# Gate logits of layer 1's row blocks: the gate's columns stationary in four column quarters, and one product that adds and turns

## The chip, the cores and the metric

One core of one Trainium2 chip runs the whole program. The metric is the device time of one launch in microseconds. Three runs of the kernel before took 630.59, 631.4 and 633.81 us, a median of 631.4.

## The reference

Chunked attention (2 batches, 8 heads, 768 positions) gives 1536 rows of 512 numbers. These go through two mixture layers of 8 experts each, whose weights are 512x1024 and 1024x512.

```python
logits = x @ w_gate                                   # layer 1, with a noise term; each row keeps its best 2 experts
h = np.maximum(x[mask] @ w1[e], 0.0)
out[mask] += top2_w[mask, k, None] * (h @ w2[e])

logits = x @ w_gate                                   # layer 2: x is layer 1's output; each row goes to its best expert
expert_idx = np.argmax(logits, axis=1)
probs = softmax(logits);  gate_w = probs[rows, expert_idx]
disp[e, counts[e]] = x[i]                             # up to `capacity` rows per expert, in row order
h = np.maximum(einsum('ecd,edf->ecf', disp, w1), 0.0);  y = einsum('ecf,efd->ecd', h, w2)
out[i] = gate_w[i] * y[expert_idx[i], pos[i]]
```

The second gate is linear in layer 1's output, so the kernel computes its logits for every expert's part of a row and lets the transfer that adds the parts in memory add the logits too.

## The kernel before, in words

**Jobs.** The expert work is a list of jobs that run one after the other: `V0`, `V8`, then `S[0]` to `S[6]` (layer 1), then `U0`, `UL` and seven more (layer 2). A job has units. A job of kind "M" has 8 units `layer1` (one 128-wide slice of the hidden layer each) and then, for each block of 128 rows, two units `rows` (the halves of the second product). `V0` is of kind "T" with one block of rows. `V8` and `S[0]` to `S[3]` are of kind "W", whose output has the rows as columns; they take their logits in `y_block` and the change doesn't touch them. `S[4]`, `S[5]` and `S[6]` are of kind "M" with three blocks of rows each. With `V0` that makes ten row blocks in layer 1.

**A row block's end.** After the second `rows` unit, `weighted` (ScalarE, L873) writes the block times its gate into `yr`. Two steps go onto a list `todo`: `row_columns` (L876) transposes `yr` on TensorE (L881) and copies the result to `yt` on ScalarE (L882); `put` calls `row_logits` and `scatter`. `row_logits` multiplies four 128x128 slices of `yt`, stationary, by the gate's 8 columns, moving, in plain fp32 into one PSUM bank (L888), and VectorE copies the 8 logits behind the row in `yr` (L889). `scatter` (L891) is an indirect transfer from GpSimd's queue that adds the block's rows to `x2_rows` in memory (L895).

**When a step runs.** `run_jobs` takes one step off `todo` after each unit in a job of kind "M" or "W" (none after the first unit, except in `S[0]`, `S[6]` and `U0`), and only steps that were there before the unit. All engines run their instructions in the order in which they were written. At the end of `S[6]` the list is emptied down to one step, which runs after `U0`'s first unit.

**What hangs on the logits.** The routing of layer 2 runs in the background in small pieces between the big products: `choose` (from unit 3 of `S[5]`), `early` (from unit 3 of `S[6]`) and `late` (from unit 3 of `U0`). Each first loads all logits with one transfer on SP's queue (L1470), which waits for all scatters written before it; then VectorE works on them (L393 on) and TensorE ranks them (L1525 in `early`, L1557 in `late`). The big products are `mm3` (L811): each operand is split into a rounded part and the rest, and three of the four products are taken; the weights come in halves that are loaded (`raww`), rounded on ScalarE (`whi`, L745) and subtracted on VectorE (`wlo`, L746). The other lines that the prediction speaks of are in the attention at the start: L242 (scores: a stationary operand of 128 rows and 64 columns, whose output goes to the lower and the upper half of the partitions in turn), L283 (64 rows and 32 columns, four places in turn), L308 (transposes) and L318 (gate logits of layer 1, of the same form as L888 but for 18 moving columns). All of these are plain fp32; in the trace such a product has two weight loads and two matmul records, and a transpose has one of each.

Of the kernel before, what the change touches and what calls it, by code (L numbers as in the profile page):

```python
# [8 lines left out]
F32 = mybir.dt.float32  # L9
# [4 lines left out]
AF = mybir.ActivationFunctionType  # L14
OP = mybir.AluOpType
AX = mybir.AxisListType
# [38 lines left out]
def attention_two_moe_kernel(  # L55
# [7 lines left out]
    nc = tc.nc  # L63
    B, H, S, D = q.shape
    NM = mem_k.shape[2]
    DM, E = w_gate1.shape
# [6 lines left out]
    KD = DM // 128  # L73
# [4 lines left out]
    W2 = DM + 8  # L78
# [24 lines left out]
    def bank(tag):  # L103
        return ps["p"].tile([128, 512], F32, name="ps" + tag, bufs=2)
# [68 lines left out]
    ident = consts.tile([128, 128], F32, name="ident")  # L173
# [10 lines left out]
    xb, st = {}, {}  # L184
# [3 lines left out]
    wg2 = consts.tile([128, KD, E], F32, name="wg2")  # L188
# [521 lines left out]
    wp = {}  # L710
# [149 lines left out]
    def rows2(n0, blk, half_, C, between=None):  # L860

        n = min(128, C - 128 * blk)
        s_ = slice(128 * blk, 128 * blk + n)
        if half_ == 0:
            st["l2"] = bank("C")
        hh, hl = st["h"]
        w = P[n0 + 2 + half_]
        mm3(st["l2"][:n], [((hh[:, 4 * half_ + f, s_], hl[:, 4 * half_ + f, s_]), (w[0][:, f], w[1][:, f]))
                           for f in range(4)], half_ == 0, half_ == 1, between, RO)

    def weighted(ps, g, n):
        yr = wp["B"].tile([128, W2], F32, name="yr", bufs=3)
        nc.scalar.activation(yr[:n, 0:DM], ps[:n], AF.Copy, scale=g[:n])  # L873
        return yr

    def row_columns(yr, n):  # L876

        p = bank("B")
        pv = p.rearrange("p (k n) -> p k n", k=KD)
        for k in range(KD):  # L880
            nc.tensor.transpose(pv[:, k, 0:n], yr[:n, 128 * k:128 * k + 128], ident[:n, :n])  # L881
        nc.scalar.activation(st["yt"][:, :, 0:n], pv[:, :, 0:n], AF.Copy)  # L882

    def row_logits(yr, n):

        p = bank("D")
        for k in range(KD):
            nc.tensor.matmul(p[:n, 0:E], st["yt"][:, k, 0:n], wg2[:, k], start=k == 0, stop=k == KD - 1)  # L888
        nc.vector.tensor_copy(yr[:n, DM:W2], p[:n, 0:E])  # L889

    def scatter(yr, n, ids_ap, first, prev):  # L891
        off = bass.IndirectOffsetOnAxis(ap=ids_ap[:n], axis=0)
        nc.gpsimd.memset(spacer, 0.0)
        if first:
            wr = nc.gpsimd.indirect_dma_start(out=x2_d, out_offset=off, in_=yr[:n], in_offset=None,  # L895
                                              compute_op=OP.add)
        else:
            wr = nc.gpsimd.indirect_dma_start(out=out, out_offset=off, in_=yr[:n, 0:DM], in_offset=None,  # L898
                                              bounds_check=N - 1, oob_is_err=False)
        for z in prev:  # L900
            tc.declare_no_dep(wr.ins, z.ins, reason="rows of other tokens")
        prev.append(wr)
# [39 lines left out]
    class Job:  # L942
# [39 lines left out]
        def rows(self, blk, half_, between=None):  # L982
            rows2(self.n0, blk, half_, self.C, between)
            if half_ == 0:
                return
            n = min(128, self.C - 128 * blk)
            yr = weighted(st["l2"], self.g[blk], n)
            if self.first:
                def put():
                    row_logits(yr, n)  # L990
                    scatter(yr, n, self.ids[blk], True, self.prev)
                self.todo += [lambda: row_columns(yr, n), put]
                return
            f = lambda: scatter(yr, n, (self.oids or self.ids)[blk], False, self.prev)
            if self.oids is None:
                self.later.append(f)
            else:
                f()
# [61 lines left out]
    def picked(b_, fl, idf, nb):  # L1060

        nv = V
        key = b_.tile([128, nv, nb], F32, name="okey")
        codes = b_.tile([128, nv * nb], F32, name="ocode")
        nc.gpsimd.iota(codes, pattern=[[-1, nv * nb]], base=nv * nb, channel_multiplier=0,
                       allow_small_or_imprecise_dtypes=True)
        cv = codes.rearrange("p (e n) -> p e n", e=nv)
        nc.vector.tensor_tensor(key, fl, cv, op=OP.mult)
        mx = b_.tile([128, 1], F32, name="omx")
        nc.vector.tensor_reduce(mx, key, axis=AX.XY, op=OP.max)  # L1070
        nc.vector.tensor_scalar(key, cv, mx[:, 0:1], None, op0=OP.is_equal)
        nc.vector.tensor_tensor(fl, fl, key, op=OP.subtract)
        se = b_.tile([128, nv], F32, name="ose")
        nc.vector.tensor_reduce(se, key, axis=AX.X, op=OP.add)
        idr = b_.tile([128, 2], F32, name="oidr")
        tr = b_.tile([128, nv, nb], F32, name="otr")
        nc.vector.tensor_tensor(tr, key, trash[:, None, 0:nb].to_broadcast([128, nv, nb]), op=OP.mult)
        nc.vector.tensor_reduce(idr[:, 1:2], tr, axis=AX.XY, op=OP.add)
        nc.vector.tensor_tensor(key, key, idf, op=OP.mult)
        nc.vector.tensor_reduce(idr[:, 0:1], key, axis=AX.XY, op=OP.add)  # L1080
        idi = b_.tile([128, 1], I32, name="oidi")
        nc.vector.tensor_tensor(idi, idr[:, 0:1], idr[:, 1:2], op=OP.add)
        return se, idr[:, 0:1], idi
# [9 lines left out]
    def rest1(wa, wb, ov, en, nb, after):  # L1093

        fl, idf, nvi = ov
        n = nc.values_load(nvi[0:1, 0:1], min_val=0, max_val=V * nb)
        b_ = wp["C"]
        with tc.If(n > 0):  # L1098
            with tc.For_i(0, n):
                se, _, idi = picked(b_, fl, idf, nb)  # L1100
                r = expert_of(b_, se, en)
                xg = b_.tile([128, 4, 256], F32, name="oraw", bufs=1).rearrange("p k f -> p (k f)")
                gather(x_d, idi[:, 0:1], xg[:, 0:W1])
                x_block(xg, 0, 128)
                g = wp["A"].tile([128, 1], F32, name="gs", bufs=10)
                gate1(xg, se, g)
                hi, lo = st["y"]

                def part(src):

                    raw = b_.tile([128, 4, 256], F32, name="oraw", bufs=1)
                    nc.sync.dma_start(raw, src)
                    nc.scalar.activation(hi[:, :, 0:256], raw, AF.Copy)
                    nc.vector.tensor_tensor(lo[:, :, 0:256], raw, hi[:, :, 0:256], op=OP.subtract)
                    return [(hi[:, k, 0:256], lo[:, k, 0:256]) for k in range(4)]

                xh, xl = st["x"]
                for f in range(4):
                    ws = part(wa[ds(r, 1)].rearrange("e (k p) f -> p (e k) f", p=128)[:, :, 256 * f:256 * f + 256])
                    ps = bank("A")  # L1120
                    mm3(ps[:, 0:256], [((xh[:, k, 0:128], xl[:, k, 0:128]), ws[k]) for k in range(KD)])
                    nc.scalar.activation(st["hr"][:, 256 * f:256 * f + 256], ps[:, 0:256], AF.Relu)
                for c in range(2):
                    turn(c, 128)
                hh, hl = st["h"]
                ps = bank("C")
                for c in range(2):
                    for j in range(2):
                        ws = part(wb[ds(r, 1)].rearrange("e (k p) f -> p (e k) f", p=128)
                                  [:, 4 * j:4 * j + 4, 256 * c:256 * c + 256])  # L1130
                        mm3(ps[:, 256 * c:256 * c + 256],
                            [((hh[:, 4 * j + k, 0:128], hl[:, 4 * j + k, 0:128]), ws[k]) for k in range(4)],
                            j == 0, j == 1)
                yr = weighted(ps, g, 128)
                row_columns(yr, 128)
                row_logits(yr, 128)
                scatter(yr, 128, idi[:, 0:1], True, [])
            after()

# [131 lines left out]
    n = 0  # L1271
# [88 lines left out]
    st["h"] = (wp["B"].tile([128, FB, CM], F32R, name="hh"), wp["B"].tile([128, FB, CM], F32R, name="hl"))  # L1360
    st["hr"] = wp["B"].tile([128, FF], F32, name="hr")
    st["yt"] = wp["B"].tile([128, KD, 128], F32, name="yt")
    st["y"] = (wp["B"].tile([128, KD, CM], F32R, name="yh"), wp["B"].tile([128, KD, CM], F32R, name="yl"))

    n2 = 4 * E
    kind1 = lambda c: "W" if c > 384 else "M"
    S = [Job(kind1(caps1[1 + s]), 4 + 4 * s, caps1[1 + s], True) for s in range(E - 1)]
# [303 lines left out]
    for job in jobs[1:-1]:  # L1671
        n = job.n0
# [60 lines left out]
```

## Time and profile before

| what | value |
|---|---|
| median of three runs | 631.4 us (630.59 to 633.81) |
| the profiled execution | 632.0 us |
| its span in the trace | 630.2 us |
| TensorE busy | 595.4 us (94%) |
| TensorE weight loads busy | 540.9 us (86%) |
| VectorE busy | 384.1 us (61%) |
| ScalarE busy | 311.2 us (49%) |
| GpSimd busy | 165.0 us (26%) |
| matmul records of L888 | 80 (8 for each of ten row blocks) |

Times in the trace count from the span's start. The 1.8 us between the span and the time of the execution lie around the span. A matmul record lasts until its last result is out, so records of consecutive matmuls overlap, and the distance from one start to the next is what a matmul costs a full engine. "Idle before" in brackets at the end of a row is the time in which that engine had nothing to run, and the arrow names what ended it.

### The profile page before, as it was taken

The numbers are of one execution on the slowest core, as the hardware profiler recorded it, in microseconds if no ns is written. First come the engines' busy times: TensorE is split into PE (matmuls) and PEld (weight loads), VectorE is DVE, ScalarE is ACT, GpSimd is POOL, SyncE is SP. The second block draws the span as 40 slices with busy tenths as digits, with TensorE's granted clock in tenths as the row PEclk, the third lists the DMA queues.
The fourth block names the chain that finished last, engine by engine and source line by source line (L and its number), as shares of the span: only waits on it lengthen the run. The fifth ranks groups of instructions, "written<-read, shape, count | busy, mean of one in ns | idle before, by whom it ended". The sixth has DMA issues, their size and how long they took to land. (4 is left out here: it accounts for less than half of the span.)

```text
span 630.2 us, 12317 instructions
## 1 busy us (share of the span) xinstructions
PE 595.4 (94%) x4523; PEld 540.9 (86%) x4529; DVE 384.1 (61%) x1015; ACT 311.2 (49%) x653; POOL 165.0 (26%) x237
## 2 busy tenths in 40 slices
PE   7699869699999999999999999999999999999996
PEld 4688657499999999999999898988979988889984
DVE  8577754677645555555555447273557648687672
ACT  5265543225544544545445435344427557686563
POOL 8894000211411312313212130302351121111201
PEclk9799886899999999999999999999999999999999
DMA  9986670339775664856536565455366486776751
GB/s 252 269 142 197 214 234 20 88 99 345 222 221 168 174 185 149 221 152 135 170 103 151 166 142 165 107 121 151 38 235 215 152 264 220 251 273 234 247 182 41
DMA packets 77068, 112.13 MB, mean 178 GB/s; under 512 B 28353, under 2 KB 28353, under 8 KB 77000
## 3 DMA queue, kind: packets, MB, share of 16 engines
q1 hardware_dynamic: 68088, 88.99, 44.7%
q0 software_dynamic: 8912, 22.28, 15.7%
q8 instruction: 38, 0.62, 0.4%
q14 instruction: 30, 0.25, 0.1%
HBM read 88.90 MB, written 22.34 MB: 176 GB/s over the span
## 5 line engine op out<-in xcount | busy, mean ns | idle before, releaser
L746 DVE TENSOR_TENSOR wlo<-raww,whi 128x512 fp32r<-128x512 f32 x254 | 168.8, 688 | 44.1 <-ACT whi L745 42.7
L745 ACT ACTIVATE whi<-raww 128x512 fp32r<-128x512 f32 x256 | 152.2, 624 | 17.7 <-DMA raww<-in_moe_w_dram 14.9
L823 DVE SCALAR_TENSOR_TENSOR hl<-psA,hh 128x384 fp32r<-128x384 f32 (+6 forms) x104 | 54.0, 519 | 80.4 <-ACT hh L822 80.0
L822 ACT ACTIVATE hh<-psA 128x384 fp32r<-128x384 f32 (+6 forms) x104 | 47.7, 458 | 109.2 <-PE psA L811 109.2
L811 PE MATMUL psA<-xh,wlo 128*128 128x256 f32 (+6 forms) x416 | 85.8, 328 | 0.8 <-ACT xh L762 0.4
L811 PE MATMUL psA<-xh,whi 128*128 128x256 f32 (+6 forms) x416 | 83.7, 322 | 0.0
L811 PE MATMUL psA<-xl,whi 128*128 128x256 f32 (+6 forms) x416 | 83.6, 323 | 0.0
L895 POOL DMA_INDIRECT x_rows<-yr,ids x25 | 39.2, 1568 | 125.4 <-ACT whi L745 86.2
L811 PEld LDWEIGHTS psA<-xh,wlo 128*128 128x128 f32 x416 | 67.7, 190 | 2.4 <-ACT xh L762 0.8
L811 PEld LDWEIGHTS psA<-xl,whi 128*128 128x128 f32 x416 | 69.3, 189 | 0.6 <-DVEq L1098 0.2
L811 PEld LDWEIGHTS psA<-xh,whi 128*128 128x128 f32 x416 | 69.1, 189 | 0.4
L751 POOL DMA_INDIRECT xg<-x_rows,ids x37 | 37.1, 1002 | 100.7 <-DVE gs L931 41.1
L811 PE MATMUL psC<-wlo,hh 128*128 128x512 f32 x200 | 57.6, 407 | 0.0
L811 PE MATMUL psC<-whi,hh 128*128 128x512 f32 x200 | 55.6, 396 | 0.0
L811 PE MATMUL psC<-whi,hl 128*128 128x512 f32 x200 | 55.0, 395 | 0.0
L763 DVE TENSOR_TENSOR xl<-psB,xh 128x512 fp32r<-128x512 f32 (+4 forms) x37 | 23.9, 645 | 43.1 <-ACT xh L762 43.1
L811 PEld LDWEIGHTS psC<-whi,hh 128*128 128x128 f32 x200 | 37.4, 189 | 8.4
L811 PEld LDWEIGHTS psC<-whi,hl 128*128 128x128 f32 x200 | 37.5, 188 | 8.3
L762 ACT ACTIVATE xh<-psB 128x512 fp32r<-128x512 f32 (+4 forms) x37 | 20.7, 560 | 44.0 <-PE psB L759 41.8
L811 PEld LDWEIGHTS psC<-wlo,hh 128*128 128x128 f32 x200 | 35.4, 189 | 5.7
L898 POOL DMA_INDIRECT out_dram<-yr,oids x13 | 13.2, 1013 | 98.1 <-ACT yr L873 71.6
L811 PE MATMUL psA<-hh,wlo 128*128 128x312 f32 (+4 forms) x160 | 36.6, 350 | 0.0
(328 smaller groups left out, 913.3 us busy)
## 6 DMA issues: line engine op xcount, KB each, us to landing
raww<-in_moe_w_dram SPq DMA_DIRECT2D x128, 512.0 KB
x_rows<-zero SPq DMA_DIRECT2D x8, 520.0 KB
raw<-in_k_dram SPq DMA_DIRECT2D x6, 512.0 KB
raw<-in_q_dram SPq DMA_DIRECT2D x6, 512.0 KB
x_rows<-xs SPq DMA_DIRECT2D x12, 256.0 KB
out_dram<-zero SPq DMA_DIRECT2D x3, 1024.0 KB
v<-in_v_dram SPq DMA_DIRECT2D x10, 256.0 KB
x_rows<-zero SPq DMA_DIRECT2D x1, 1042.0 KB
```

The lines of the kernel that those rows point to most:

```text
L745: nc.scalar.activation(hi[:, c], raw, AF.Copy)
L746: (eng or nc.vector).tensor_tensor(lo[:, c], raw, hi[:, c], op=OP.subtract)
L751: return nc.gpsimd.indirect_dma_start(out=xg, out_offset=None, in_=src, in_offset=bass.IndirectOffsetOnAxis(ap=ids_ap, axis=0))
L762: nc.scalar.activation(xh[:, :, o], pv[:, :, 0:n], AF.Copy)
L763: low = lambda: nc.vector.tensor_tensor(xl[:, :, o], pv[:, :, 0:n], xh[:, :, o], op=OP.subtract)
L811: nc.tensor.matmul(ps, w[a], x[b], start=first and i == 0, stop=last and i == n - 1)
L822: nc.scalar.activation(hh[:, f, 0:C], ps[:, 0:C], AF.Relu)
L823: nc.vector.scalar_tensor_tensor(hl[:, f, 0:C], ps[:, 0:C], 0.0, hh[:, f, 0:C], op0=OP.max, op1=OP.subtract)
L895: wr = nc.gpsimd.indirect_dma_start(out=x2_d, out_offset=off, in_=yr[:n], in_offset=None, compute_op=OP.add)
L898: wr = nc.gpsimd.indirect_dma_start(out=out, out_offset=off, in_=yr[:n, 0:DM], in_offset=None, bounds_check=N - 1, oob_is_err=False)
```

## The change

Nine of the ten row blocks get three steps in place of two: `columns`, `parts`, `put`. `parts` takes the four slices of `yt` as moving operands (128 columns each) against four slices of the gate, stationary, 32 columns each (8 of the gate and 24 zeros), each at its own quarter of the array's columns, so that the four results lie in four quarters of the partitions of one bank; ScalarE copies them to a new tile `lp`. `put` then makes one product with `lp` stationary and a constant `pick` (128x8, a one where the partition's number within its quarter is the column's number) moving: it adds the four quarters and turns the result to rows. Since a block now has three steps and two units, `columns` first runs the `put` of the block before it if that is the last step on the list. The last block of `S[6]` keeps the old two steps and the old product. `lp`, `wgz` and `pick` are set up once, when the pools of the expert work open.

```diff
-    def row_logits(yr, n):
+    def row_parts(n):
         p = bank("D")
         for k in range(KD):
-            nc.tensor.matmul(p[:n, 0:E], st["yt"][:, k, 0:n], wg2[:, k], start=k == 0, stop=k == KD - 1)
-        nc.vector.tensor_copy(yr[:n, DM:W2], p[:n, 0:E])
+            nc.tensor.matmul(p[32 * k:32 * k + 32, 0:n], st["wgz"][:, k], st["yt"][:, k, 0:n], start=True, stop=True,
+                             tile_position=(0, 32 * k))
+        nc.scalar.activation(st["lp"][:, 0:n], p[:, 0:n], AF.Copy)
+        return p
+
+    def row_logits(yr, n, p):
+        if p is None:
+            p = bank("D")
+            for k in range(KD):
+                nc.tensor.matmul(p[:n, 256:256 + E], st["yt"][:, k, 0:n], wg2[:, k], start=k == 0, stop=k == KD - 1)
+            nc.vector.tensor_copy(yr[:n, DM:W2], p[:n, 256:256 + E])
+            return
+        nc.tensor.matmul(p[:n, 256:256 + E], st["lp"][:, 0:n], st["pick"], start=True, stop=True)
+        nc.vector.tensor_copy(yr[:n, DM:W2], p[:n, 256:256 + E])
...
             if self.first:
+                got, before = [], self.todo.pop() if self.todo else None
+
+                def columns():
+                    if before is not None:
+                        before()
+                    row_columns(yr, n)
+
+                def parts():
+                    got.append(row_parts(n))
+
                 def put():
-                    row_logits(yr, n)
+                    row_logits(yr, n, got.pop() if got else None)
                     scatter(yr, n, self.ids[blk], True, self.prev)
-                self.todo += [lambda: row_columns(yr, n), put]
+                self.todo += [columns, put] if self is S[-1] and blk == self.nb - 1 else [columns, parts, put]
...
+    st["lp"] = wp["B"].tile([128, 128], F32, name="lp")
+    st["wgz"] = wp["B"].tile([128, KD, 32], F32, name="wgz")
+    st["pick"] = wp["B"].tile([128, E], F32, name="pick")
+    nc.gpsimd.memset(st["wgz"], 0.0)
+    nc.gpsimd.tensor_copy(st["wgz"][:, :, 0:E], wg2)
+    nc.vector.tensor_reduce(st["pick"], ident.rearrange("p (k c) -> p c k", k=KD)[:, 0:E], axis=AX.X, op=OP.max)
```

## Rows read from the trace of the kernel before

**Rows 1.** Busy time by stretch: PE, PEld, DVE, ACT, POOL, clock, DMA share, GB/s.

```profile
400.00:425.00 25.00, 24.50 (x151) 23.33 (x150) 13.68 (x34) 10.40 (x20) 3.16 (x3) 1.00 0.48 111
425.00:450.00 25.00, 25.00 (x174) 22.36 (x173) 10.06 (x23) 11.83 (x24) 8.62 (x9) 1.00 0.52 117
```

**Rows 2.** Timeline of PE, 340 us on, a row with a wait.

```profile
420.39 0.17 PE L1525 MATMUL psD<-em,tri 128*128 128x12 bf16 x1 [0.51 <-DVE em L1521]
```

**Rows 3.** The line of the old product, its matmuls by form.

```profile
L888 PE MATMUL psD<-wg,yt x80: 169/256/257, 131.6 to 443.7; 128*128 128x8 f32 x80
```

**Rows 4.** Timeline of PE (start, us from first start to last end), units 1 to 3 of `S[6]`.

```profile
403.44 0.60 PE L881 MATMUL psB<-ident,yr 128*128 128x128 f32 x4
403.79 0.95 PE L811 MATMUL psA<-xh,wlo 128*128 128x384 f32 x4
...
405.28 0.86 PE L811 MATMUL psA<-xh,whi 128*128 128x384 f32 x4
405.98 0.95 PE L888 MATMUL psD<-wg,yt 128*128 128x8 f32 x8
406.79 0.94 PE L811 MATMUL psA<-xh,wlo 128*128 128x384 f32 x4
...
408.98 0.86 PE L811 MATMUL psA<-xh,wlo 128*128 128x384 f32 x4
```

**Rows 5.** Timeline of PE in the attention.

```profile
61.75 1.11 PE L283 MATMUL psC<-v,ex 64*32 64x65 f32 x64
62.79 0.66 PE L308 MATMUL psD<-ident,xs 128*128 128x128 f32 x4
63.28 0.97 PE L318 MATMUL psD<-wg,xt 128*128 128x18 f32 x8
64.18 1.15 PE L242 MATMUL psA<-kt,qz 128*64 128x64 f32 x32
```

**Rows 6.** Timeline of PE at the end of `S[6]`.

```profile
439.26 1.07 PE L811 MATMUL psC<-whi,hl 128*128 128x512 f32 x4
440.17 0.95 PE L888 MATMUL psD<-wg,yt 128*128 128x8 f32 x8
441.11 0.66 PE L881 MATMUL psB<-ident,yr 128*128 128x128 f32 x4
```

**Rows 7.** Timeline of ACT in the same stretch.

```profile
440.37 0.69 ACT L873 ACTIVATE yr<-psC,gs 128x512 f32<-128x512 f32 x1 [1.54 <-PE psC L811]
441.87 0.60 ACT L882 ACTIVATE yt<-psB 128x512 f32<-128x512 f32 x1 [0.81 <-PE psB L881]
443.23 0.38 ACT L822 ACTIVATE hh<-psA 128x256 fp32r<-128x256 f32 x1 [0.76 <-PE psA L811]
```

**Rows 8.** Timeline of DVE, POOL and SP's queue: `S[5]`'s last block, `early`, `late`.

```profile
407.17 0.15 DVE L889 COPY yr<-psD 128x8 f32<-128x8 f32 x1
408.06 1.56 POOL L895 DMA_INDIRECT x_rows<-yr,ids  x1 [4.13 <-ACT whi L745]
409.70 0.56 DVE L823 SCALAR_TENSOR_TENSOR hl<-psA,hh 128x384 fp32r<-128x384 f32 x1 [1.77 <-ACT hh L822]
412.83 0.37 SPq L1470 DMA_DIRECT2D lg<-x_rows  x1
417.14 0.25 DVE L393 TENSOR_REDUCE fm_m<-lg 128x12 f32<-128x96 f32 x1
...
449.76 0.37 SPq L1470 DMA_DIRECT2D lg<-x_rows  x1
452.23 0.25 DVE L393 TENSOR_REDUCE fm_m<-lg 128x12 f32<-128x96 f32 x1
```

**Rows 9.** Line L895 from 340 to 450 us: from issue to landing.

```profile
DMA to landing us min/median/max: 4.6/4.8/5.7
```

**Rows 10.** Timelines of POOL and PE at the start of the expert work.

```profile
110.62 0.57 POOL L561 TENSOR_TENSOR gt<-oh,gw 128x63 f32<-128x63 f32 x2 [27.80 <-DVE gw L544]
...
135.31 0.51 PE L458 MATMUL psD<-oh_R,oh_L 128*128 128x108 f16 x7 [1.06 <-DVE oh_L L448]
```

More of the change, by code (lines that the diff above doesn't have):

```diff
@@ L1135, in rest1 @@
                 row_columns(yr, 128)
-                row_logits(yr, 128)
+                row_logits(yr, 128, None)
                 scatter(yr, 128, idi[:, 0:1], True, [])
```

## The prediction

> **What bounds the kernel now.** I read the busy time by stretch first, over the stage that holds nine of the ten blocks. TensorE is busy 24.5 and 25.0 us of each 25 there, at a granted clock of 1.00, and no other engine passes 14 [rows 1]. Then I read TensorE's timeline from 340 us on for rows with a wait. Of the stage in question only one is there: 0.51 us before L1525, ended by VectorE's routing chain in `early` [rows 2]. So in this stage a microsecond taken from TensorE's stream is a microsecond of the kernel, and two places matter besides: that wait, and the end of `S[6]`, where steps that normally lie a unit apart run one behind the other. Last I read what the chain behind the wait hangs on: VectorE's copy of the last logits of `S[5]`, its scatter, the load of all logits, VectorE's first reduction [rows 8].
>
> **The old product.** 80 records are 8 for each of ten blocks [rows 3]. In the full stream they cost more than their records show: the next group starts 0.81 us after the first of them, and then takes 0.94 us where an undisturbed one takes 0.86 [rows 4]. That is 0.81 + 0.08 = 0.89 us per block, or 0.11 us per record, for 8 moving columns: what is paid is the eight 128-column weight loads. In the blocks changed, this goes.
>
> **`parts`.** The four quarters need two passes each of 128 moving fp32 columns. One pass of that length costs what a transpose does, 0.35 us to the next group's start plus 0.09 of its lengthening (0.95 against 0.86), over four: 0.11 us [rows 4]. How much the quarters overlap is not shown for this form, so I take the nearest two. L242 with two column halves: 32 records in 1.15 us are at most 0.036 each, where one pass of 64 columns alone would be half of 0.11, 0.055. L283 with four places: 64 records in 1.11 us are at most 0.017 each, again against 0.055, so at least 3.2 of 4 run together [rows 5]. Bounds for the eight records are 0.22 us (all four together, twice 0.11) and 0.88 us (one by one). L283 is nearest in the number of places, L242 in the number of rows; I take 0.22, and 0.44 (two at a time) stays in the range.
>
> Going in and out of the divided array costs something too. Going in: eight records of L318 in a stream would let the next start after 0.81 us as L888 does [rows 4], at 64.09; L242 starts at 64.18, 0.09 later [rows 5]. Ahead of `parts` stands mostly a group of 512 columns. There four take 1.07 us and the next group starts after 0.91 [rows 6], so the pitch is 0.23, a record lasts 1.07 - 3 x 0.23 = 0.38, and waiting for its end rather than its place costs 0.15. Coming out: L308 starts 0.07 us before the end of L283's last record and its four take 0.66 us where undisturbed ones take 0.60 [rows 4, 5]; in the whole array a group starts about 0.16 us before the end of the one before it (439.26 + 1.07 against 440.17) [rows 6]. So coming out costs 0.09 + 0.06 = 0.15 us. I add 0.05 for the first quarter weights, which nothing hides after a stop; zero and 0.1 bound that. Together `parts` is 0.15 + 0.22 + 0.05 + 0.15 = 0.57 us, call it 0.6.
>
> The Trainium skill, page "TensorEngine Tiling (Array Packing)", section "Tiling Modes", has a rule against the change: going from one division of the array to another drains TensorE, where going from tile to tile does not. The trace agrees with it (64.18 where 64.09 was due, and the longer transposes after L283), and by that rule the product pays two drains per block that the old one did not; without it the sum per block would be 0.3 us lower.
>
> **`put`'s product.** One fp32 product with a 128-column stationary operand and 8 moving columns is the old product's form with a quarter of its records: 0.89 / 4 = 0.22 us. Its operand `lp` was written a unit before, so it waits for nothing except at the end of `S[6]`. Per block the sum is 0.6 + 0.22 = 0.82 against 0.89: 0.07 us gained. Seven blocks (three of `S[4]`, three of `S[5]`, the first of `S[6]`) give 0.5 us. `V0`'s block counts as nothing: right behind it TensorE waits 1.06 us for VectorE [rows 10], and 0.1 us either way ends in that wait. The last block of `S[6]` is unchanged.
>
> **ScalarE's copy to `lp`.** 128x512 takes 0.60 us and 128x256 0.38 [rows 7], so 128x128 takes about 0.27, nine times 2.4 us. ScalarE is busy 10 to 12 us of 25 [rows 1], and behind the copy stand `whi` roundings that are used units later: nothing on the path, except here:
>
> **The end of `S[6]`.** Its second block's `parts` comes right after the last unit, and its `put` stands at the head of the third block's `columns`, with no unit in between. The copy to `lp` is behind `weighted` on ScalarE, which ends at 440.37 + 0.69 = 441.06 [rows 7]; then 0.27 us of copy, then 0.22 us of product: the transposes start at about 441.6 where they start at 441.11 now [rows 6]. That costs 0.5 us once, and everything later moves with it. Bounds: 0.3, and 1.0 if `parts` itself ends last.
>
> **The logits of `S[5]`'s last block.** `put` goes from the second to the third unit of `S[6]`. VectorE's copy is at 407.17 now; the new product follows the unit that ends at 408.98 [rows 4], and the copy comes behind the `hl` of that unit, at 409.70 + 0.56 = 410.26 [rows 8], 3.1 us later. The scatter follows 0.89 us after the copy and lands after 4.8 us [rows 8, 9] (408.06 + 4.8 is the 412.83 of the load, which so waits for it): the load goes from 412.83 to 415.9. How long it takes is bounded by `late`, where the reduction runs 2.47 us after the issue [rows 8]. The reduction could thus run at 418.4, not 417.14: 1.3 us late. Behind it VectorE is idle some 0.7 us before the next `hl` (417.39 to 418.11, were it ready), which takes that back; 0.6 us stays and lengthens the wait before L1525 from 0.51 to 1.1 us [rows 2]. Bounds: nothing, if the load lands in about a microsecond; 2.4 us, if all 4.31 us from issue to reduction were needed. `S[4]`'s last block moves by as much ahead of `choose`, whose result no TensorE wait hangs on; SP's queue holds its next weight loads up to 3 us longer there, and no TensorE row of the stage waits for weights. In `late` nothing moves against the rest, for the last block keeps its place.
>
> **Setup.** A small reduction on VectorE and two small writes on GpSimd, which is idle 27.80 us up to 110.62 [rows 10]: nothing.
>
> **Sum.** -0.5 + 0.5 + 0.6 = +0.6 us. The profiled execution took 632.0 us, so 632.6 for one like it; the median of the runs is 0.6 lower, which gives 632.0 us against 631.4. Under 0.5% (3.2 us) a measurement of this kernel can't tell a change from none; that is the line for "faster" and "slower" below.
>
> **Rivals.**
> A: the quarters run together and the stops cost nothing. `parts` is 0.25, the block 0.47, seven blocks gain 7 x 0.42 = 2.9; with the two losses 629.6 us. For it: L283's 64 records in 1.11 us. Against it: the gaps before L242 and after L283. The same page of the Trainium skill, "TensorEngine Tiling (Array Packing)", section "Performance Considerations", advises just this exchange of operands for a product of at most 32 moving columns.
> B, on the slow side: the quarters of 128 rows don't run together. `parts` is 0.88 + 0.35 = 1.23, the block 1.45, seven blocks lose 7 x 0.56 = 3.9; at the end of `S[6]` `parts` now ends last (1.0), and 0.6: +5.5, 636.9 us. It decides once the eight records take over about 0.75 us. Against it: L242, also of 128 rows, overlaps two.
> C: the load of the logits is really needed that long, and the wait before L1525 grows by 2.4 us, not 0.6: 633.8 us. For it: nothing on VectorE's timeline shows when the load landed. Against it: `late`'s 2.47 us.
> D: the quarters run two at a time, as L242's halves: `parts` 0.44 + 0.35 = 0.8, the block 1.02, 7 x 0.13 = 0.9 lost; 0.5 at the end and 0.6 make +2.0 to 633.4 us.
>
> **How the numbers follow.** Forecast 0.52 (its own range 631.0 to 633.0), A 0.14, B 0.10, C 0.12, D 0.12. The range runs from 629.8, which leaves out half of A, to 635.0, which leaves out B: about 0.17 outside. Faster by over 0.5% (under 628.2) needs A without the two losses: 0.04. Slower by over 0.5% (over 634.6) is B and the upper part of C and D: 0.14. Within 0.5%: 0.82.
>
> **What would show it.** In the trace after, 72 records of the quarters and 18 of the last product in place of 72 of L888's 80; eight quarter records from first start to last start in about 0.15 us (forecast), 0.35 (D) or 0.8 (B); a gap of about 0.15 us on either side; the group behind the last product lengthened as behind L888. The wait before L1525 should be near 1.1 us, with the load near 415.9, and the transposes at the end of `S[6]` about 1.4 us behind the last unit's end, not 0.94. I am wrong if TensorE's waits elsewhere in layer 2 change, since nothing of the change reaches there but a shift in time.

## The result, and the profile after

The changed kernel takes 638.8 us against 632.1 us in the same series (medians of six runs each). By the medians it is slower by 6.6 us; by the ratio of the runs, 1.0137 (1.0104 to 1.017), by 6.6 to 10.7. The forecast was 632.0 us, and the time lies above its range.

| | before | after |
|---|---|---|
| profiled execution, its span (us) | 632.0, 630.2 | 641.5, 639.7 |
| TensorE busy (us) | 595.4 | 596.8 |
| ScalarE busy (us) | 311.2 | 313.2 |
| VectorE busy (us) | 384.1 | 383.5 |
| instructions | 12317 | 12373 |

TensorE is busy 1.4 us longer in a span that is 9.5 us longer: most of the loss is idle time (time at a low clock counts as busy). I located it by the start of one and the same instruction group in both timelines; the difference is called the shift below. Five points tell most of it:

| group | before | after | later by |
|---|---|---|---|
| first group behind the transposes of `V0`'s block | 129.76 | 130.45 | 0.69 |
| last unit of `V8` | 144.18 | 145.06 | 0.88 |
| fourth group behind `S[0]`'s first transposes | 146.91 | 152.55 | 5.64 |
| transposes of `S[4]`'s first block | 350.59 | 355.91 | 5.32 |
| first group of `U0`, behind `S[6]` | 441.53 | 447.67 | 6.14 |

The first 0.69 us lies ahead of any instruction that was moved, and it is not the added setup's either: at the transposes of `V0`'s block, kernels below with the same setup stand between 1.29 us ahead of the kernel before and 0.53 behind. Of the rest, 4.8 us is lost within 8 us, at the first transposes of `S[0]`, 200 us ahead of the stage that the forecast was about. Both are in layer 1. TensorE's timeline there, before (start, us, engine, line, operation, tile):

```profile
144.18 0.74 PE L811 MATMUL psA<-hh,whi 128*128 128x312 f32 x4
144.75 0.60 PE L759 MATMUL psB<-ident,xg 128*128 128x128 f32 x4
145.11 0.81 PE L811 MATMUL psA<-hh,wlo 128*128 128x312 f32 x4
...
146.91 0.73 PE L811 MATMUL psA<-hh,wlo 128*128 128x312 f32 x4
```

and after, from the product of L458 on (in brackets the idle time and what ended it):

```profile
135.99 0.51 PE L458 MATMUL psD<-oh_R,oh_L 128*128 128x108 f16 x7 [1.38 <-DVE oh_L L448]
...
145.06 0.73 PE L811 MATMUL psA<-hh,whi 128*128 128x312 f32 x4
149.03 1.12 PE L759 MATMUL psB<-ident,xg 128*128 128x128 f32 x4 [3.24 <-DMA xg<-x_rows,ids]
149.80 1.39 PE L811 MATMUL psA<-hh,wlo 128*128 128x312 f32 x4
...
152.55 0.73 PE L811 MATMUL psA<-hh,wlo 128*128 128x312 f32 x4
```

A wait of 3.24 us for gathered rows is new, and the groups behind it take 1.12 us for 0.60 and 1.39 for 0.81. From 144.18 to 144.75 is 0.57 us, from 145.06 to 149.03 it is 3.97: 3.40 us from the wait. From 144.75 to 146.91 is 2.16 us, from 149.03 to 152.55 it is 3.52: 1.36 us from slower groups. The granted clock stands in the ninth place of the windows, 1.00 before and 0.52 after (about the lower of the two levels, 1.2 GHz); before:

```profile
144.00:147.00 3.00, 3.00 (x24) 3.00 (x23) 2.71 (x9) 2.26 (x5) 1.58 (x3) 1.00 0.99 270
```

after:

```profile
149.00:152.00 3.00, 2.97 (x13) 2.97 (x14) 1.09 (x4) 1.63 (x3) 1.03 (x2) 0.52 0.90 286
```

Why the gathers are late is in the queues. Before, the scatter of `V0`'s block, the first of the four gathers for `S[0]`, and SP's zero fills of the tensor that the scatter writes to:

```profile
136.53 1.63 POOL L895 DMA_INDIRECT x_rows<-yr,ids_e  x1 [16.69 <-issue]
138.47 1.00 POOL L751 DMA_INDIRECT xg<-x_rows,ids  x1 [0.30 <-issue]
...
141.32 0.97 SPq L1239 DMA_DIRECT2D x_rows<-zero  x2
```

after, with VectorE's copy of the logits:

```profile
135.85 12.78 SPq L1262 DMA_DIRECT2D x_rows<-zero  x2
137.90 0.15 DVE L902 COPY yr<-psD 128x8 f32<-128x8 f32 x1
143.05 1.63 POOL L908 DMA_INDIRECT x_rows<-yr,ids_e  x1 [22.87 <-DVE f L681]
144.98 1.00 POOL L751 DMA_INDIRECT xg<-x_rows,ids  x1 [0.31 <-DVE f L696]
...
149.10 0.95 POOL L751 DMA_INDIRECT xg<-x_rows,ids  x1 [0.30 <-issue]
```

A row of SP's queue marked x2 holds two fills: before, they are issued at 141.32 and 141.74; after, at 135.85 and 148.25. Fills and scatter write rows of the same tensor, `x2_rows`, so whichever is written down first goes first. `V8` issues five fills of 520 KB. The first is far ahead of the scatter in both kernels (112.04 and 113.12). Before, `V0`'s `put` ran ahead of the hook that issues the second; the scatter went 0.97 us after its copy (135.56, 136.53) and the fill waited for it. With one step more in `V0`'s list, `put` runs behind that hook. Now the second fill goes first, at 135.85, and the scatter goes only 5.15 us after its copy; the third waits for the scatter in its turn. The DMA engines, busy with the fill and the weights issued before it, fell idle at about 141.5, 1.6 us ahead of the scatter; what passes in these 1.6 us the rows don't show. The gathers need nothing of either, but stand behind the scatter in GpSimd's queue: the first goes at 144.98 instead of 138.47, the last at 149.10 instead of 145.37. The releaser printed for the scatter (`DVE f L681`, 22.87 us) isn't the real one: on a wait for several semaphores, where the engine named had long been done, it was a DMA.

The part that the forecast was about went nearly as forecast. The quarters and the last product, lines by form:

```profile
L888 PE MATMUL psD<-yt,wgz x72: 272/285/298, 132.3 to 446.2; 128*32 128x128 f32 x72
...
L901 PE MATMUL psD<-pick,lp x18: 170/256/277, 136.8 to 447.2; 128*128 128x8 f32 x18
...
L890 ACT ACTIVATE lp<-psD x9: 269/270/279, 132.8 to 446.7; 128x128 f32<-128x128 f32 x9
```

and on TensorE's timeline, `S[4]`'s first block (it answers to [rows 4, 6]):

```profile
355.91 0.60 PE L881 MATMUL psB<-ident,yr 128*128 128x128 f32 x4
...
358.65 1.09 PE L811 MATMUL psC<-whi,hl 128*128 128x512 f32 x4
359.67 0.43 PE L888 MATMUL psD<-yt,wgz 128*32 128x128 f32 x8
360.02 1.20 PE L811 MATMUL psC<-wlo,hh 128*128 128x512 f32 x4
361.06 1.09 PE L811 MATMUL psC<-whi,hh 128*128 128x512 f32 x4
361.98 1.08 PE L811 MATMUL psC<-whi,hl 128*128 128x512 f32 x4
362.90 0.28 PE L901 MATMUL psD<-pick,lp 128*128 128x8 f32 x2
363.03 0.63 PE L881 MATMUL psB<-ident,yr 128*128 128x128 f32 x4
```

The eight records last 0.43 us together and 0.28 each, so 0.15 to 0.16 us lie between first and last start: the four quarters run together. `parts` costs 0.35 us to the next start, 0.10 going in (1.02 us from 358.65 to 359.67, where an undisturbed group of this kind takes 0.92) and 0.12 coming out (1.04 us to 361.06, for 0.92): 0.57 us. The last product costs 0.13 and 0.05 on the transposes behind it (0.40 us to 363.43, for 0.35): 0.18. Before, the same groups stood at 350.59, 356.98 (ahead of the next transposes) and 360.18; after at 355.91, 361.98 and 365.36. The shift goes from 5.32 by 5.00 to 5.18: this block gains 0.14 us.

From `S[4]` to `S[6]` there are three new or longer waits, at the end of `S[4]`, in `early` and at the end of `S[6]`:

```profile
367.76 0.97 PE L811 MATMUL psA<-xh,wlo 128*128 128x384 f32 x4 [0.94 <-ACTq L1121]
...
426.25 0.18 PE L1554 MATMUL psD<-em,tri 128*128 128x12 bf16 x1 [1.30 <-DVE em L1550]
...
446.02 0.43 PE L888 MATMUL psD<-yt,wgz 128*32 128x128 f32 x8
447.03 0.39 PE L901 MATMUL psD<-pick,lp 128*128 128x8 f32 x2 [0.59 <-ACT lp L890]
447.27 0.64 PE L881 MATMUL psB<-ident,yr 128*128 128x128 f32 x4
...
472.18 0.66 PE L759 MATMUL psB<-ident,xg 128*128 128x128 f32 x4 [2.38 <-DMA xg<-x_rows,ids_ul]
```

They come back in the points below. The last row, at the start of `UL`, is why this execution is longer than the median: the wait was 0.94 us in the execution shown of before, and the clock falls behind it once more (0.62 from 472 to 475). From 6.14 us at `U0` the shift grows to 9.0 by 476 us. Four of the six runs of the changed kernel took 638.1 to 638.8, two 641.5 and 642.5, of which this is one.

### The profile page after: what moved, and what is told of

Read it like the earlier page. It is cut to its first block, busy times and chain, and to the rows that moved or that the text cites. A ratio compares the mean times of both kernels' runs of the same rounds, so it can differ in the third digit from the quotient of the medians.

```text
span 639.7 us, 12373 instructions
## 1 busy us (share of the span) xinstructions
PE 596.8 (93%) x4541; PEld 537.5 (84%) x4547; DVE 383.5 (60%) x1016; ACT 313.2 (49%) x662; POOL 165.6 (26%) x239
```

## The experiments

Theory: the loss is `V0`'s scatter, which the extra step put behind a zero fill, and with it the gathers queued behind it (theory 1 where an expectation numbers them). The main rivals: the divided products themselves cost it, or the late load of the logits in `early`. The chip that ran these gave medians of 631.5 us for the kernel before, in both batches, and spread more than the first, so intervals are some 0.7% wide.

**`V0`'s block alone in the old form.**

```diff
- [columns, put] if self is S[-1] and blk == self.nb - 1 else [columns, parts, put]
+ [columns, put] if self is V0 or self is S[-1] and blk == self.nb - 1 else [columns, parts, put]
```

> The changed kernel, with V0's one row block put back to its two steps and the old product; the eight blocks of the S jobs stay changed. Theory 1 (the loss is V0's put, one unit of V8 later: its scatter comes to stand behind a zero fill of the same rows, and the gathers for S[0] stand behind the scatter in GpSimd's queue): the 3.24 us wait of TensorE before S[0]'s first transposes goes, and the slow stretch of the clock after it; about 5.3 us come back, 633.4 us, that is 0.5 to 1.3 us over the kernel before, for the end of S[6] and the later load of the logits. Rival 2 (the quarters and the broken stream in the S jobs cost the time): V0's block is one of nine, so under 1 us comes back, 638 us.

634.2 us, ratio 1.0043 (1.0007 to 1.0078): 2.7 us (0.4 to 4.9) over the kernel before, where the whole change had cost 6.6. By the medians 3.9 us came back, where 5.3 were expected. Timelines of GpSimd and PE:

```profile
135.72 1.63 POOL L908 DMA_INDIRECT x_rows<-yr,ids_e  x1 [16.75 <-issue]
...
156.56 1.17 PE L811 MATMUL psA<-hh,wlo 128*128 128x312 f32 x4 [2.56 <-DVE yl L839]
```

The scatter is back, the gathers run from 137.66 to 144.56, and `S[0]`'s first transposes at 143.94 wait for nothing. So by the medians `V0`'s block, one of nine, carries more than half of the loss. What remains is more than the 0.8 us that the first profile shows from `S[4]` to `S[6]`, though 0.8 lies inside the interval. The profiled execution, the longest of the twelve (638.8 us), lost most of its time elsewhere: 4.3 us at the second row, where ScalarE had waited 5.96 us for weights and a clock of 0.5 followed, and 2.5 at the start of `UL`. At the same place the profiles of the two versions below that concern `S[5]`'s last block lost 2.0 us each; one of them is the kernel before in this stretch, so the loss needs none of the change.

**The delay without the quarters.** The kernel before, with one empty step ahead of `V0`'s `put`:

```diff
- self.todo += [lambda: row_columns(yr, n), put]
+ self.todo += [lambda: row_columns(yr, n)] + [lambda: None] * (self is V0) + [put]
```

> The kernel before, with one empty step between V0's columns and V0's put, so that the old product and the scatter come one unit of V8 later; nothing else is changed, no quarters anywhere. Theory 1: the scatter waits for the zero fill as in the changed kernel (GpSimd's queue idle until about 142 us), TensorE waits about 3 us before S[0]'s transposes, and 4.5 to 5.5 us are lost: 637 us. Rival 2: the form of the product is what costs, so this stays at 632.1 us, within 0.5.

637.2 us, 1.0094 (1.0059 to 1.0128): +5.9 us with no new instruction at all. Timelines of PE, SP's queue and GpSimd:

```profile
134.42 12.39 SPq L1239 DMA_DIRECT2D x_rows<-zero  x2
134.57 0.51 PE L458 MATMUL psD<-oh_R,oh_L 128*128 128x108 f16 x7 [1.93 <-DVE oh_L L448]
...
136.28 1.39 PE L811 MATMUL psA<-xh,wlo 128*128 128x312 f32 x4
...
141.47 1.64 POOL L895 DMA_INDIRECT x_rows<-yr,ids_e  x1 [22.39 <-DVE ce L706]
...
149.12 0.66 PE L759 MATMUL psB<-ident,xg 128*128 128x128 f32 x4 [2.51 <-DMA xg<-x_rows,ids]
```

Fill (the first of the two in its row), scatter and the wait before L759 stand as in the changed kernel, the wait somewhat shorter, and the gathers run from 143.41 to 147.21. That settles that at `S[0]` the order is the cause and not the divided array. It is not a clean copy, though: here the old product also moves from ahead of the product of L458 to behind it, so TensorE comes to that wait earlier (1.93 us instead of 1.06) and then has three groups at 1.23 to 1.39 us for 0.73, at a granted clock of 0.50. In this profile that adds 2.4 us (the shift goes from -0.74 at 134.57 to +1.66 at 139.54), and `S[0]` adds 4.3 (to 5.96 at 153.43). So part of the 5.9 us is not the scatter's.

**The fill later instead of the scatter earlier.** The changed kernel, with the fills from the second on one unit later:

```diff
- hook(V8, j - 2, lambda j=j: blank_rows(*zeros[(j + 2) % len(zeros)]))
+ hook(V8, j - 2 if j == 3 else j - 1, lambda j=j: blank_rows(*zeros[(j + 2) % len(zeros)]))
```

> The changed kernel with V8's zero fills from the second on written one unit of V8 later, so that again only one of them stands ahead of V0's scatter, as in the kernel before; V0's scatter keeps its later place. Theory 1: the scatter follows VectorE's copy at about 138.8 us and S[0]'s first gather is at about 140.8, 2.3 us later than in the kernel before, which had about 2.6 us of slack there; TensorE waits at most 0.5 us: 633.4 to 634.4 us. Rival 3 (the one unit of delay alone makes the gathers late, whatever stands in front of the scatter): the wait of about 3 us stays, 638 us.

636.5 us, 1.0069 (1.0045 to 1.0093). Timelines of GpSimd, SP's queue and PE:

```profile
138.72 1.63 POOL L908 DMA_INDIRECT x_rows<-yr,ids_e  x1 [18.71 <-issue]
...
146.43 2.31 SPq L1262 DMA_DIRECT2D x_rows<-zero  x3
148.99 5.10 SPq L728 DMA_DIRECT2D raww<-in_moe_w_dram  x3
...
161.21 1.03 PE L811 MATMUL psA<-xh,wlo 128*128 128x432 f32 x4 [1.35 <-ACT xh L762]
...
423.62 0.18 PE L1554 MATMUL psD<-em,tri 128*128 128x12 bf16 x1 [1.57 <-DVE em L1550]
```

The scatter follows its copy at once and `S[0]` doesn't wait, as theory 1 says. The time is a miss all the same (633.4 to 634.4 was expected): the fills, bunched now, stand ahead of weight loads on SP's queue, ScalarE waits 3.4 us twice for those weights where it waited 2.4 and 2.2 before, and the shift grows by 1.45 us to 2.41 at 161.21. That the bunched fills are to blame is argued, not shown: three other profiles lost 2.0 to 4.3 us in this stretch with the fills in their old places. The wait in `early` adds 2.65 us (shift 2.18 to 4.83), with 1.57 us of wait and a granted clock of 0.50 from 425 to 427.

**The scatter behind the gathers.** The changed kernel, `V0`'s block by the old product, its `put` six units later:

```diff
+ if self is V0:
+     self.todo += [columns] + [lambda: None] * 6 + [put]
+     return
```

> The changed kernel with V0's block on the old product and its put six units later still, behind unit 7 of V8 where the gathers for S[0] have been written. Theory 1: the scatter still waits for the fills, but nothing that TensorE needs stands behind it in GpSimd's queue, so TensorE does not wait before S[0]: 633.4 us, as with V0's block put back. Rival 4 (the late scatter or the fills delay the gathers in memory or in the transfer engines, not in GpSimd's queue): TensorE waits as in the changed kernel or longer, 638 us or more.

635.5 us, 1.0053 (1.0021 to 1.0085). Timelines of GpSimd and PE:

```profile
137.67 0.94 POOL L751 DMA_INDIRECT xg<-x_rows,ids  x1 [17.97 <-DVE ids L661]
145.40 0.65 PE L759 MATMUL psB<-ident,xg 128*128 128x128 f32 x4
152.60 1.64 POOL L908 DMA_INDIRECT x_rows<-yr,ids_e  x1 [6.23 <-DMA raww<-in_moe_w_dram]
...
421.53 0.18 PE L1557 MATMUL psD<-em,tri 128*128 128x12 bf16 x1 [1.55 <-DVE em L1553]
```

Here the scatter is 16 us later than before, and `S[0]`'s transposes don't wait. Just before them TensorE is 0.38 us earlier than in the kernel before, and at 160 us 0.38 later; the old product, which now runs in between, costs 0.89. So the late scatter itself costs nothing that shows; what costs is what was queued behind it. That is theory 1's sharpest test, and it holds. The 3.4 us (1.3 to 5.4) of the whole are over the 0.5 to 1.3 expected with `V0`'s block put back; this profile has its loss in `early`, a wait of 1.55 us and a low clock behind it (shift 0.10 to 2.72).

**`S[5]`'s last block in the old form too**, which takes the delayed load out of `early`:

```diff
- self is V0 or self is S[-1] and blk == self.nb - 1
+ self is V0 or self in S[-2:] and blk == self.nb - 1
```

> The changed kernel with V0's block and the last block of S[5] on the old two steps, so that the load of the logits for `early` keeps its old place; seven blocks stay changed. Theory 5 (of what V0's block does not explain, the larger part is the wait before TensorE ranks in `early`, and the half-speed clock that follows it in some executions): the wait falls from 1.3 to 1.6 us back to about 0.5, no half-speed stretch follows, and the time is 0.5 to 1.0 us over the kernel before (the ends of S[4] and S[6]). Rival 6 (the quarters cost it, a little in each block): with seven of eight blocks left it stays 2.5 to 3 us over the kernel before.

632.3 us, 1.0009 (0.9984 to 1.0035): +0.8 us by the medians, as expected. The interval (-1.0 to 2.2 us) excludes rival 6, but not that nothing is lost, and it overlaps that of `V0`'s block alone. The wait in `early` is what it was, no stretch of low clock follows, and from `S[4]`'s first block to `U0` the shift grows only from 0.46 to 0.63:

```profile
420.73 0.18 PE L1554 MATMUL psD<-em,tri 128*128 128x12 bf16 x1 [0.52 <-DVE em L1550]
```

**The late load without the quarters.** The kernel before, with an empty step ahead of that block's `put`:

```diff
+ [lambda: None] * (self is S[-2] and blk == self.nb - 1) + [put]
```

> The kernel before with one empty step between columns and put of S[5]'s last block, so that its logits, its scatter and the load of all logits come one unit later; no quarters anywhere. Theory 5: TensorE's wait in `early` grows from 0.5 to about 1.5 us, and in some executions the clock falls to half behind it: 1 to 2.7 us over the kernel before. Rival 6: no change, within 0.5 us.

630.8 us, 0.9979 (0.9951 to 1.0007): no loss, against an expected one of 1 to 2.7 us.

```profile
418.39 0.17 PE L1525 MATMUL psD<-em,tri 128*128 128x12 bf16 x1 [0.88 <-DVE em L1521]
```

The step alone moves VectorE's copy of the logits by 2.1 us (from 5.93 to 8.03 us behind `S[6]`'s start) and the wait by 0.37. In the changed kernel the copy is at 8.77, since the last product follows a unit and the copy goes behind that unit's `hl`, and the wait is 1.30 to 1.57 us. So this expectation failed: the delay of one step isn't worth a microsecond by itself. That the wait in `early` explains what `V0`'s block doesn't is thus not shown: taking the delay away fits it, bringing it in alone does not.

**Quarters only where no joint follows**, five blocks (first and third of `S[4]`, first two of `S[5]`, first of `S[6]`), the old form elsewhere:

```diff
+ def old(i):
+     return self is V0 or (self, i) in ((S[4], 1), (S[5], 2), (S[6], 1), (S[6], 2))
...
- [columns, put] if self is S[-1] and blk == self.nb - 1 else [columns, parts, put]
+ [columns, put] if old(blk) else [columns, parts, put]
```

> Quarters only where nothing else moves: S[4]'s first and last block, S[5]'s first two, S[6]'s first; V0's block, S[4]'s second, S[5]'s last and S[6]'s last two keep the old two steps in their old places. Theory 1 and 5 together: the waits of the changed kernel before S[0], in `early`, at the end of S[4] and at the end of S[6] are gone, and each of the five blocks gives about 0.1 us: 0.5 us under the kernel before, which is less than the interval. Rival 6: 1.5 us or more over it.

631.4 us, 1.0012 (0.9985 to 1.0039). From `S[4]`'s first block to `U0` the shift falls from 0.48 us to 0.13. Five gains of 0.14 would give twice as much, but the wait at the end of `S[4]` is not gone, though the second block has the old product there. Later a wait for gathered rows, at a place where the kernel before has one too, takes more than all of it:

```profile
362.93 0.97 PE L811 MATMUL psA<-xh,wlo 128*128 128x384 f32 x4 [0.51 <-ACTq L1123]
...
466.95 0.63 PE L759 MATMUL psB<-ident,xg 128*128 128x128 f32 x4 [3.09 <-DMA xg<-x_rows,ids_ul]
```

In this execution the second wait cost 3.7 us with the low clock behind it. No version measurably beats the kernel before.

## Why the prediction was wrong

**The step that failed: "`V0`'s block counts as nothing: right behind it TensorE waits 1.06 us for VectorE [rows 10], and 0.1 us either way ends in that wait".** I priced the block on TensorE alone, and there it does cost little: the shift is 0.69 us ahead of it and 0.88 behind (143.92 for 143.04), and the wait grew to 1.38. But `put` also issues a scatter, one unit later than before, and I never asked what had been written down for the scatter's tensor and for GpSimd's queue in that unit. The fill and the gathers were both in the code. For `S[5]`'s last block I followed the scatter and the load behind it; in `V8`, where `V0`'s `put` runs beside fills and gathers, I didn't. The runs put 4.8 us of the profile there (3.40 of wait, 1.36 of clock). The wait goes with the old form (2.7 us left of 6.6), comes back without the quarters, and is gone when the scatter goes behind the gathers. My sign of being wrong named TensorE's waits in layer 2, and this one is in layer 1, so the sign didn't cover it. In layer 2 the wait at the start of `UL` grew too, from 0.94 to 2.38 us, but in kernels with the same code there it ranges from 0.9 to 3.1.

**The end of `S[4]`: a term left out.** I named the end of `S[6]` as the only place where steps follow without a unit between. `S[4]` ends in the branch of `rest1` (L1121), at which all engines meet. From the group ahead of its second block's `parts` to the first behind the branch is 2.40 us (365.36 to 367.76) for 2.03 (360.18 to 362.21): 0.37 lost, though `parts` takes 0.35 us there instead of 0.81. The two groups behind it are 0.14 us shorter than behind the old product, and the last product adds its 0.18, so the shift goes from 5.18 to 5.59 (373.39 for 367.80) and this block loses 0.41. The wait of 0.94 us is ended by ScalarE, which comes to the branch behind `weighted` and the copy to `lp` (0.69 and 0.27). That the copy is the cause is not shown: with five blocks there is no copy in this place, and the distance is 2.40 us all the same (360.53 to 362.93). There ScalarE's load of the branch's number takes 0.95 us, for 0.47 before and 0.48 after; why stays open.

**`parts` and the last product: right as a sum.** 0.57 us measured for 0.57 forecast, 0.18 for 0.22; a full block gains 0.14 for 0.07. That `parts` fits to the hundredth is in part luck, for its terms don't. Split as above, the stops are 0.10 and 0.12 for 0.15 each. The rule of the Trainium skill, page "TensorEngine Tiling (Array Packing)", section "Tiling Modes", that a new division of the array drains TensorE, agrees with these two numbers. The quarters are then 0.35 for 0.22 and 0.05. Split as in the prediction, which counts the next group's late start as part of the stop (it starts 0.08 us before the last quarter's end, where the whole array has 0.16), coming out is 0.20 and the quarters 0.27. Rival A, without stops, fell with them; so did B and D, by the 0.16 us from first to last start.

**The copy to `lp` and the end of `S[6]`: right.** 0.27 us as forecast. From the group ahead of `parts` to the first of `U0` is 2.67 us (445.00 to 447.67) for 2.27 (439.26 to 441.53): +0.40, for 0.5.

**The load in `early`: the size nearly right, its consequence not seen.** Copy, scatter, load and first reduction after (it answers to [rows 8]):

```profile
415.01 0.15 DVE L902 COPY yr<-psD 128x8 f32<-128x8 f32 x1
415.91 1.56 POOL L908 DMA_INDIRECT x_rows<-yr,ids  x1 [3.77 <-DVE wlo L746]
421.25 0.37 SPq L1499 DMA_DIRECT2D lg<-x_rows  x1
423.86 0.25 DVE L393 TENSOR_REDUCE fm_m<-lg 128x12 f32<-128x96 f32 x1 [1.58 <-DMA lg<-x_rows]
```

The reduction now waits for the load, 2.61 us after its issue, near the 2.47 of `late` that I took for it. Measured from the start of `S[6]` it is 1.7 us later (1.3 forecast), and the wait before L1525 is 1.30 us (1.1 forecast). Rival C, with 2.4 us more, fell with that. In two of the four profiles that have this delay in full, this wait was 1.55 and 1.57 us and the clock fell behind it, which I had no term for.

**Together from `S[4]` to `S[6]`:** six blocks at -0.14, `S[4]`'s second +0.41, `early` +0.79, `S[6]`'s end +0.40 make +0.76; the shift grows from 5.32 to 6.14, by 0.82. The forecast of this stage was +0.6. That it came so near is partly luck: the gains were twice as large as taken, and `S[4]`'s end, which was not in the sum, took that back. The rest of the 6.6 us is 4.8 at `S[0]`, and about a microsecond that no profile places; waits that vary by more than that between executions are behind `S[0]`'s transposes, in `early` and in `UL`.

**Open.** How often weights come late behind `S[0]`'s transposes, how often the clock falls behind the waits in `early` and `UL`, and so how much of the 2.7 us with the old form in `V0` is theirs; the intervals overlap. And what delays ScalarE at the end of `S[4]` without a copy there.

## What to carry to other kernels

A step that is moved by one slot moves everything it issues: for each DMA in it, list who writes the same tensor and who stands behind it on the same queue in the slot that it leaves and in the one that it enters. An exchange that gains 0.14 us a block on the full stream lost 0.4 at each of the two places where the next step follows without cover, so joints are counted one by one, not as one more block. And a wait is priced with what follows it: here the time behind the wait of 3.24 us cost 1.4 us more.

## What the runs showed that I had not expected

Behind waits of 1.55 to 3.24 us TensorE often went on at a granted clock near 0.5 for some 3 us: 3.24 (after, `S[0]`), 2.38 (after, `UL`), 2.51 and 1.93 (the delay without quarters), 1.57 and 1.55 (`early`), 2.56 and 1.93 (`S[0]` and `UL`, `V0`'s block in the old form), 3.09 (`UL`, five blocks). Behind waits of 1.30 (`early`, after), 1.38 (L458, after) and 1.31 (`UL`, scatter behind the gathers) it went on at full pace; but so it did behind 1.95 (L458, scatter behind the gathers) and 1.74 (`UL`, the delay without quarters). At L458 1.93 us in one execution and 1.95 in another were followed by different clocks, so the length of a wait alone doesn't tell what follows. The gather of `UL` alone made waits of 0.9 to 3.1 us in kernels whose code there is the same, and late weights behind `S[0]`'s transposes cost 0 to 4.3 us, so single executions differ by up to 4 us where the code does not.
